# Sliding-window attention and a ReGLU layer: the planner replaced by a written-out sequence, and the second layer of tile 1 by seven block products

## The chip, the core and the metric

The kernel runs on one core of one Trainium2 chip. The metric is the device time of one execution in microseconds (us), of which several runs are taken. A profile of one execution stands beside it: its span runs from the first to the last instruction on the core, and its own time is a little longer than that span. The engines are PE (TensorE, with its weight loads listed apart as PEld), DVE (VectorE), ACT (ScalarE), POOL (GpSimd) and SP (SyncE, which here only issues transfers).

## The reference

Two steps follow each other, with float32 inputs and output.

```python
# q, k, v: [8, 8, 576, 64] (batch, heads, sequence, head size)
scores = 0.125 * q @ k.T                    # per batch and head
mask   = (rel >= 0) & (rel < 64)            # rel = position of query - position of key
attn   = softmax(where(mask, scores, -1e9)) @ v
x      = attn.transpose(0, 2, 1, 3).reshape(4608, 512)
out    = (relu(x @ w_gate) * (x @ w_val)) @ w_out     # w_gate, w_val [512, 1536], w_out [1536, 512]
```

Each query sees itself and the 63 positions before it. The second step is most of the arithmetic: three matrix products over 4608 tokens.

## The kernel before, in words

**Tiles.** The 4608 tokens are cut into 9 tiles of 512 (t = 0 to 8; `LAST` is 8). A tile holds eight windows of 64 queries, and as a batch has nine windows, tile t takes most of its windows from batch t and the rest from its neighbour. Everything on SBUF is float16, apart from the tiles `pr` (128x512 float32, twelve of them) in which partial results wait. PSUM has eight banks of 128x512 float32: seven form the pool "bank", one the pool "bo".

**Attention of a tile** (`attend_tile`). GpSimd loads k and q (`qk_load`, L386), VectorE turns them (`qk_trans`, L392). `score_run` (L416, L424) makes the scores of eight windows for one half of the heads in four banks; ScalarE takes the exponential (L684) into four of the ten tiles `p`. v is loaded by GpSimd's queue in several transfers (`v_load`, L395) into every second window block, and the blocks between are filled from there: by a copy on an engine for batches 0 and 1 (`v_copy`, L647 to L655), and from batch 2 on by a transfer from SBUF to SBUF that SP issues (`v_move`, L659). `value_block` (L430) multiplies the weights with v; the 32 blocks of a tile go into five banks of 7, 7, 7, 7 and 4 (`value_bank`), 28 or 16 small products each. Column 64 of each block is the sum for the softmax: VectorE takes its reciprocal (L699), multiplies (`norm`, L437) and turns the result into `xs`, x transposed (`turn`, L442).

**First layer.** Tile 0 takes it directly (`direct_halves`, L836, for the start; `direct_block`, L789). Tiles 1 to 8 take it by block products (`fast_hidden`, L924): each operand is a 2x2 of blocks, and seven products P1 to P7 of sums and differences of blocks stand in for eight. The x sums are made per tile (`x_form`, L755, on POOL or in part DVE), the sums of w_gate and w_val once (`w_form`, L873, on POOL or DVE). Products that are used twice are copied out of PSUM by ScalarE (`snap`, L933), added by VectorE (`sum`, L940), passed through relu on ScalarE (L949), multiplied on POOL (`mult`, L958) into `g_sb`.

**Second layer.** `output` (L998) does it directly: for each of four groups of 128 tokens, twelve products of 512 columns, an evacuation by ScalarE (L1009) and a 256 KB store by SP (L1013). `fast_output` (L1037) does it by seven block products of 2 x 6 matmuls of 256 columns (L1088): four sums of g (`g_sum`, L1056, DVE, the last of them also POOL), three copies by ScalarE (L1099), three additions by VectorE (`osum`, L1124), an evacuation (L1127) and stores (L1069). It needs sums of w_out, made once (`w_sums`, `wo_form`, L1032, DVE or POOL). In tile 8 the last block leaves in three pieces: 128 KB, 64 KB and 64 KB (L1111, L1116), the second issued by ScalarE's queue, the other two by SP. Which tiles take which form is set by one number:

```python
TF = int(K["TF"])                          # L1133; 2 before
...
if t < TF:
    output(t, lambda sub, j: ..., range(4))
else:
    fast_output(t, lambda i: ...)
```

**What sets the order.** `first_part` is written out by hand. `second_part` builds some 1640 operations with a name, the engines that may run each (with a duration for each), the operations that it follows and the buffers that it takes and gives back. A planner (`Plan`) then goes through modelled time: whenever an engine is free by its model, `pick` takes the ready operation of the smallest key, `grab` gives it buffers, and `emit` issues its instructions. The keys come from the numbers in `K`, with corrections per tile. The planner has its own model of the transfers (`flow`, `transfer`) and of the fetching of PE's instructions (`fetch`). The instructions of each engine run in the order in which they were emitted; between engines they wait on semaphores. Loads share GpSimd's in-order queue, stores and v moves share SP's.

Of the kernel before, what the change touches and what calls it, by code (L numbers as in the profile page):

```python
# [20 lines left out]
K = {"T1": 49.924, "STEP": 29.94, "wo1": 20.947, "wo2": 27.392, "q0": 0.81, "q1": 2.61, "q10": 3.105, "q11": -1.419, "v": -0.6, "v1": -2.289, "ql": 1.41, "qt": 0.88, "qti": 4.69, "vl": 0.91, "vc": 0.04, "vm": 1.83, "e": 7.62, "gap": 3.77, "gap1": 7.386, "r": -6.21, "tn": 1.66, "xf": 4.78, "wf": -35.503, "wfj": -20.847, "sn": 2.67, "su": -2.15, "re": 17.5, "mu": -6.61, "la": -4.79, "o0": 4.313, "o0j": 21.729, "o0s": -0.33, "oo": 0.007, "os": 0.386, "oj": 4.81, "gs": -1.18, "fo": 0.015, "fi": 0.098, "fs": 4.74, "fu": 0.27, "W0": 119.46, "TF": 2, "rs": 5.846, "rv": 1.504, "rt": 0.895, "wl": -5.903, "wln": 11.853, "l0": -6.097, "l1": 7.146, "lv": -0.183, "lvs": 3.345, "wo0": 16.427, "db": -13.173, "di": -0.612, "dv": 3.665, "slack": 0.5, "d2": 2.074, "bl": 9.0, "lv0": 12.142, "d": {'2:xf': -6.976, '2:gap': 2.801, '2:su': -6.005, '3:r': 8.222, '5:tn': 4.276, '6:fi': -0.099, '7:q0': -4.657, '6:su': 3.912, '6:qti': 7.826, '6:mu': 3.718, '7:e': 6.275, '7:r': 4.193, '1:r': 13.271, '2:vl': 6.019, '3:su': 0.149, '6:gs': -0.12, '6:vm': -0.213, '7:qt': -0.899, '6:re': 13.416, '7:qti': -0.543, '7:su': 1.652, '8:v': -2.013, '8:e': -0.256, '0:r': -1.206, '0:fi': 0.02, '1:os': -0.217, '0:mu': 1.725, '2:q0': 1.741, '2:qt': 1.317, '4:e': -3.039, '3:qt': -1.647, '5:fi': -0.024, '4:tn': -0.784, '6:ql': -0.117, '6:os': -0.156, '5:vl': -3.703, '6:gap': -0.68, '7:gap': -0.33, '7:vl': 1.061, '8:gs': 2.641, '8:mu': -3.707, '0:oj': 0.301, '1:xf': 1.119, '0:la': -0.276, '0:e': 0.153, '0:v': -1.992, '0:ql': 0.562, '0:vc': -0.21, '0:os': 0.264, '0:vm': -3.122, '0:gap': -0.425, '0:su': -2.2, '0:fu': 0.645, '0:qti': 2.927, '0:q0': -0.308, '0:fo': 0.017, '0:q1': 1.371, '0:tn': -0.43, '0:gs': 0.145, '0:oo': -0.005, '0:qt': -0.234, '0:vl': -0.08, '1:gap': 3.317, '0:xf': 0.894, '1:su': 0.479, '0:re': 3.598, '1:qt': 0.476, '1:oj': 1.108, '1:qti': -0.592, '1:re': -4.458, '2:v': -0.349, '2:fs': -4.83, '1:sn': -1.051, '1:fs': 0.31, '2:vm': -1.579, '1:fi': -0.01, '1:fo': -0.048, '2:fu': -2.569, '1:v': 0.852, '1:oo': -0.029, '1:q0': 0.371, '2:fo': -0.012, '1:tn': 0.283, '1:mu': 0.421, '2:os': 0.099, '1:e': 1.753, '1:q1': 0.357, '1:ql': 0.301, '2:vc': 0.095, '3:fi': -0.026, '2:ql': -0.412, '3:fo': -0.13, '2:tn': -1.562, '3:tn': 1.005, '2:la': -0.315, '2:mu': -1.84, '3:qti': -1.366, '3:e': 3.975, '3:fs': -0.171, '2:re': 1.299, '2:fi': 0.003, '3:gs': 2.169, '3:sn': -1.944, '2:gs': -0.762, '2:oo': 0.02, '3:q0': 0.206, '2:sn': -0.542, '2:e': 1.079, '3:q1': -0.835, '3:vc': 0.13, '2:q1': 0.676, '3:xf': -0.808, '4:qti': 1.269, '4:v': -0.286, '4:q0': -1.124, '4:la': 0.685, '3:ql': -0.066, '3:vl': -0.069, '3:la': 0.114, '3:mu': -0.69, '3:fu': -0.034, '4:fi': -0.002, '4:fo': -0.035, '4:os': 0.034, '3:re': -1.107, '3:v': -0.668, '3:os': 0.038, '4:q1': -0.644, '4:re': 10.33, '4:fs': 0.147, '4:sn': -0.236, '4:r': -0.56, '5:e': -4.75, '4:mu': -1.436, '5:sn': -0.929, '5:fo': 0.022, '4:fu': 1.111, '5:oj': -0.83, '4:xf': -0.115, '5:v': -3.283, '5:re': 1.853, '5:gs': 1.765, '5:la': 2.425, '5:oo': -0.102, '5:os': 0.039, '4:oj': 0.107, '5:fs': -0.393, '4:oo': 0.002, '5:xf': 0.475, '5:gap': 0.037, '4:gap': 0.009, '4:vm': -0.251, '4:vl': -0.186, '5:vc': -1.079, '5:su': -1.334, '6:xf': -3.246, '6:fo': 0.058, '6:e': 3.933, '5:q1': 0.282, '5:vm': 0.736, '5:fu': 0.612, '6:tn': -0.333, '6:oo': -0.064, '6:q1': 0.038, '6:vc': -0.831, '5:qt': -0.35, '6:fs': -1.242, '5:ql': 0.14, '5:q0': -0.526, '6:vl': -0.535, '6:fu': -0.538, '5:mu': -0.49, '5:r': -0.711, '7:gs': -1.426, '6:v': -0.377, '7:tn': -0.762, '7:oo': 0.079, '7:vm': 0.69, '7:fs': 0.778, '7:fi': 0.0, '6:r': 0.133, '7:v': -1.49, '6:qt': -0.711, '6:q0': -0.395, '7:ql': 0.339, '6:sn': 0.042, '8:su': -1.663, '8:os': 0.104, '8:tn': 1.195, '8:q1': 1.664, '7:fu': -0.818, '7:os': -0.003, '8:fu': -0.594, '7:q1': 0.55, '8:fo': 0.075, '7:mu': -0.507, '7:xf': 0.075, '8:gap': -0.962, '7:vc': 0.072, '8:vm': -0.773, '8:vc': -1.223, '7:sn': 0.05, '8:vl': -0.544, '8:xf': -0.329, '8:oj': -0.046, '7:fo': 0.002, '7:oj': 0.682, '8:qti': -0.921, '8:fs': -1.361, '8:re': -0.296, '8:oo': 0.012, '8:la': 0.307, '7:re': -1.461, '8:fi': 0.008, '8:qt': -0.143, '8:q0': 0.588}, "pads": 78, "cap": 4.8}  # L21


PLANS = []


class Op:


    def __init__(self, name, key, engines, fn, after, take, give, dma):  # L30
        self.small = 0
        self.count = 0
        self.opens, self.closes = None, False
        self.name = name
        self.key, self.engines, self.fn = key, engines, fn
        self.take, self.give, self.dma = take, give, dma
        self.left = len(after)
        self.feeds = []
        self.ready = dict.fromkeys(engines, 0.0)
        self.end = None  # L40
        self.on = None


class Plan:


    LAG = {"PE": 0.055, "ACT": 0.035, "DVE": 0.035, "POOL": 0.075, "SP": 0.06}
    DRAIN = 0.2
    AHEAD = 20.0
    TURN = 0.093  # L50
    LIMIT = 1e9
    FLIGHT = 8
    STAY = 4.0
    ASK = 165
    NEED = 445

    def __init__(self, free, queue, pools):
        self.free = dict(free)
        self.queue = queue
        self.pools = {name: [(t, n, item) for n, (t, item) in enumerate(items)] for name, items in pools.items()}  # L60
        self.home = {id(x[2]): name for name, items in self.pools.items() for x in items}
        self.open = []
        self.known = {e: [] for e in free}
        self.waiting = {e: [] for e in free}
        self.times = []
        self.port = {"DVE": 0.0, "POOL": 0.0}
        self.small = False
        self.at = 0
        self.asked = self.got = 0
        self.come = []  # L70
        self.flight = [None] * self.FLIGHT
        self.moved = 10.0
        self.jobs = {"q": [[10.0, queue["q"] - 10.0, "q", None]], "sp": []}
        self.n = 0
        self.all = []
        self.log = []

    def op(self, name, key, engines, fn, after=(), take=(), give=(), dma=None):
        after = [a for a in dict.fromkeys(after) if a is not None]
        o = Op(name, key, engines, fn, after, take, give, dma)  # L80
        self.n += 1
        o.n = self.n
        self.all.append(o)
        for a in after:
            a.feeds.append(o)
        return o

    def know(self, o):
        for e in o.engines:
            self.known[e].append(o)  # L90
            heapq.heappush(self.times, o.ready[e])

    def fetch(self, n, t, dur, keep):
        at, asked, got, come = self.at, self.asked, self.got, list(self.come)
        end = at + n
        while True:
            ask, need = 256 * asked + self.ASK, 256 * got + self.NEED
            nxt = min(ask, need, end)
            t += (nxt - at) * dur / n
            at = nxt  # L100
            if at == end:
                break
            if ask <= need:
                begin = max([t] + come[-1:])
                begin += max(0.4, min(K["cap"], self.queue["q"] - begin), min(2.0, self.queue["sp"] - begin))
                come.append(begin + 2.4 + K["slack"])
                asked += 1
            else:
                t = max(t, come[got])
                got += 1  # L110
        if keep:
            self.at, self.asked, self.got, self.come = at, asked, got, come
        return t
# [6 lines left out]
    def flow(self, jobs, now, until):  # L120
        done = []
        while now < until and any(jobs.values()):
            act = {w: j[0] for w, j in jobs.items() if j and j[0][0] <= now + 1e-9}
            after = min([until] + [j[0][0] for j in jobs.values() if j and j[0][0] > now + 1e-9])
            if not act:
                now = after
                continue
# [1077 lines left out]
```

## Time and profile before

| | before |
|---|---|
| median of 3 runs | 306.01 us (305.54 to 306.56) |
| the profiled execution: its time | 305.09 us |
| its span | 303.1 us |
| mean granted TensorE clock | 0.997 |
| POOL busy | 231.5 us (76%), 233 instructions |
| HBM read, written | 37.75 MB, 9.44 MB |
| DMA on the whole | 32.87 MB, mean 108 GB/s |

The busy lines and the stages that the prediction rests on are shown there. How to read them: a row of busy times gives what an engine was working on, not whether the end waited for it; the chain of waits, followed back from the last instruction, says that. An engine that is busy 97% of the span can lose time only in the places where its rows have gaps, and most of the gaps of this profile lie ahead of 66 us. Line numbers in the rows are those of the kernel before.

### The profile page before, as it was taken

How to read it: one execution, taken by the hardware profiler on the slowest of the kernel's cores; microseconds unless marked ns; L12 is line 12 of the kernel's file. 1: busy time of each engine (PE TensorE's matmuls, PEld its weight loads, DVE VectorE, ACT ScalarE, POOL GpSimd, SP SyncE). 2: the span in 40 equal slices, each digit the busy share in tenths (PEclk: the TensorE clock that was granted, in tenths of full speed). 3: DMA queues.
4: the chain of work that ended last, by engine and by line, in shares of the span. 5: the costliest groups of instructions: out<-in, count | busy, mean ns of one | idle time of the engine just before them, and what ended most of it. 6: DMA issues, size and time to landing. Idle time of an engine off the chain costs nothing.

```text
span 303.1 us, 11292 instructions
## 1 busy us (share of the span) xinstructions
PE 294.5 (97%) x4793; PEld 242.5 (80%) x4793; DVE 252.6 (83%) x428; ACT 213.1 (70%) x415; POOL 231.5 (76%) x233
## 2 busy tenths in 40 slices
PE   7799999999999999999999999999999999999994
PEld 5576655778767888888888888888888888888884
DVE  5879999999967988998869998889978688776962
ACT  4464426898588788785866987977588858887731
POOL 8698757999997999799558976699559567948630
PEclk9999999999999999999999999999999999999998
DMA  7999999992599916933979835343931112001024
GB/s 216 186 190 205 196 193 218 182 200 44 37 151 155 165 45 83 145 41 53 207 167 114 116 54 98 76 86 36 118 92 38 40 37 69 2 0 37 19 75 151
DMA packets 59586, 32.87 MB, mean 108 GB/s; under 512 B 39440, under 2 KB 54416, under 8 KB 59536
## 3 DMA queue, kind: packets, MB, share of 16 engines
q0 software_dynamic: 46672, 18.29, 51.6%
q1 hardware_dynamic: 12720, 13.80, 14.5%
q8 instruction: 37, 0.61, 0.9%
q14 instruction: 13, 0.11, 0.1%
q10 hardware_dynamic: 144, 0.07, 0.1%
HBM read 37.75 MB, written 9.44 MB: 156 GB/s over the span
## 4 chain that ended last, share of the span: by engine, by line
PE 89%; DMA 7%; DVE 1%; issue 1%; POOL 1%; ACT 0%; SPq 0%; ACTq 0%; DVEq 0%; POOLq 0%
PE bank L924 46%; PE bank L1088 21%; PE bank L998 6%; PE bank L789 5%; PE bank L430 4%; DMA q<-in_q_dram 3%; PE bank L424 2%; DMA v<-in_v_dram 2%; PE bank L836 2%; DMA v<-v 2%; PE bank L416 2%; DVE qT L392 0%; DVE v L512 0%; POOL k L386 0%; POOL v L395 0%
## 5 line engine op out<-in xcount | busy, mean ns | idle before, releaser
L958 POOL TENSOR_TENSOR g_sb<-pr,pr 128x512 f16<-128x512 f32 x96 | 121.1, 1277 | 37.8 <-ACT pr L949 9.1
L940 DVE TENSOR_TENSOR pr<-bank,pr 128x512 f32<-128x512 f32 x144 | 92.4, 680 | 20.2 <-PE bank L924 15.1
L933 ACT COPY pr<-bank 128x512 f32<-128x512 f32 x144 | 80.8, 590 | 23.1 <-PE bank L924 20.6
L924 PE MATMUL bank<-xt,us 128*128 128x256 f16 x384 | 56.1, 273 | 0.1
L924 PE MATMUL bank<-xt,vs 128*128 128x256 f16 x384 | 55.7, 273 | 0.0
L949 ACT ACTIVATE pr<-pr 128x512 f32<-128x512 f32 x72 | 44.9, 638 | 4.7 <-DVE pr L940 4.5
L684 ACT ACTIVATE p<-bank 128x512 f16<-128x512 f32 (+1 forms) x68 | 36.4, 591 | 10.0 <-PE bank L424 9.9
L924 PE MATMUL bank<-xt,wg 128*128 128x256 f16 x288 | 42.8, 273 | 0.1
L924 PE MATMUL bank<-xt,wv 128*128 128x256 f16 x288 | 42.8, 273 | 0.0
L924 PEld LDWEIGHTS <-vs 128*128 128x128 f16 x384 | 37.3, 98 | 5.3
L924 PEld LDWEIGHTS <-us 128*128 128x128 f16 x384 | 36.8, 98 | 5.1 <-issue 0.3
L395 POOL DMA_DIRECT2D v<-in_v_dram x40 | 35.1, 881 | 1.5 <-DMA wo<-in_moe_w_out_dram 1.1
L1088 PEld LDWEIGHTS <-g_sb 128*128 128x128 f16 x336 | 32.5, 98 | 3.9
L1088 PE MATMUL bank<-wo,g_sb 128*128 128x256 f16 x252 | 32.6, 273 | 0.0
L971 ACT ACTIVATE pr<-bank 128x512 f32<-128x512 f32 x48 | 27.5, 602 | 6.1 <-PE bank L924 4.8
L924 PEld LDWEIGHTS <-wv 128*128 128x128 f16 x288 | 27.7, 98 | 4.5
L924 PEld LDWEIGHTS <-wg 128*128 128x128 f16 x288 | 27.7, 98 | 4.1 <-DVE xt L442 0.4
L437 DVE TENSOR_TENSOR xw<-bank,r 128x448 f16<-128x448 f32 (+2 forms) x45 | 25.8, 574 | 1.6
L1088 PEld LDWEIGHTS <-ss 128*128 128x128 f16 x252 | 24.5, 98 | 3.0
L442 DVE STREAM_TRANSPOSE xt<-xw 128x512 f16<-128x512 f16 (+2 forms) x38 | 24.9, 669 | 0.4
L998 PE MATMUL bank<-wo,g_sb 128*128 128x512 f16 x96 | 23.9, 380 | 0.0
L1088 PE MATMUL bank<-ts,ss 128*128 128x256 f16 x168 | 21.8, 273 | 0.0
(103 smaller groups left out, 388.3 us busy)
## 6 DMA issues: line engine op xcount, KB each, us to landing
out_dram<-pr SPq DMA_DIRECT2D x35, 256.0 KB, 2.8
k<-in_k_dram POOLq DMA_DIRECT2D x15, 288.0 KB, 6.5
q<-in_q_dram POOLq DMA_DIRECT2D x15, 288.0 KB, 6.9
v<-in_v_dram POOLq DMA_DIRECT2D x32, 128.0 KB, 5.3
v<-v SPq DMA_DIRECT2D x12, 132.0 KB, 2.7
v<-v SPq DMA_DIRECT2D x24, 66.0 KB, 3.4
wg<-in_moe_w_gate_dram POOLq DMA_DIRECT2D x6, 256.0 KB, 6.6
wv<-in_moe_w_val_dram POOLq DMA_DIRECT2D x6, 256.0 KB, 8.7
```

Of the source, the lines that this page charges most:

```text
L395: nc.gpsimd.dma_start(v16s[b % 2][lo:hi, g, :, 0:64], v[b, :, 64 * g - 64 + lo:64 * g - 64 + hi].rearrange("h p d -> p h d"))
L437: nc.vector.tensor_tensor(x, blocks_of(to, n)[:, :, 0:D].rearrange("p s (c e) -> p s e c", e=2), r[:, :, :, None].to_broadcast([128, n, 2, ...
L442: nc.vector.transpose(xt[:, 2 * hh:2 * hh + 2, c0:c0 + n].rearrange("p e (s c) -> p s e c", c=32), x)
L684: nc.scalar.activation(pp[g][:, 0:n].rearrange("p n c -> p (n c)"), st[g][:, 0:64 * n], ACT.Exp, scale=scale)
L924: nc.tensor.matmul(slot[to][:, HT * m:HT * m + HT], w[:, kk, 128 * m:128 * m + 128], x[:, kk], start=(first and m == 0 and kk == 0), stop= ...
L933: lambda e, hold=hold, slot=slot: nc.scalar.copy(hold["x"], slot["A"]),
L940: nc.vector.tensor_tensor(hold["x"], slot[to], hold["x"], ADD)
L949: lambda e: nc.scalar.activation(hold["x"], hold["x"], ACT.Relu), after=[o])
L958: lambda e: VEC[e].tensor_tensor(gh[:, fs:fs + 2, h], pair(a["x"]), pair(b["x"]), MUL),
L971: lambda e, hold=hold, slot=slot, i=i: nc.scalar.activation(hold["x"], slot["A"], ACT.Copy if i else ACT.Relu),
L998: nc.tensor.matmul(bank["b"][:, 0:c1 - c0], gs[t % 2][:, f, 128 * sub:128 * sub + 128], wo[:, f, c0:c1], start=(j == 0 and i == 0), stop=( ...
L1088: nc.tensor.matmul(bank[to][:, HD * m:HD * m + HD], a[:, f, 128 * m:128 * m + 128], b[:, f], start=(first and m == 0 and f == 0), stop=(f ...
```

## The change

The planner is gone. In its place stands a string `ORDER` of 1641 steps. A step is the number of an operation (in the order in which the code creates them), a letter for the engine that runs it (P, A, D, G for POOL, S for SP), and a digit for each buffer that it takes. `Plan.run` walks through the string, asserts that everything that an operation follows has been issued and that its buffers are free, and issues it. So the order on every engine, the engine of each operation that may run on several, and the buffers are all written out.

`TF` goes from 2 to 1: tile 1 takes its second layer by seven block products too, so that `output` is left for tile 0 alone and the sums of w_out are needed one tile earlier. The other numbers in `K` change as well; under the written order they only feed keys that nothing reads. `value_bank` can put two banks in one operation, which the number `pair` = 0 leaves off, and the number of tiles `p` is now read from `K` (ten, as before). `first_part` and the bodies of all operations are as they were.

The written order differs from the planner's on every engine. Counted in operations: the five value banks of each tile and the two of tile 0 stand in 18 separate stretches on PE where there were 29; of the 24 sums of w_gate and w_val, 15 run on DVE and 9 on POOL (18 and 6 before), of the 12 sums of w_out 7 and 5 (4 and 8), of the 32 x sums 6 and 26 (8 and 24), and of the copies of v, ScalarE makes 6 (3) and DVE 2 (5). On PE the second operation after the hand-written part is now the second half of a contraction of tile 0 whose first half stands ahead of it. On SP the last steps are the 64 KB piece (step 1640), two 256 KB stores (1628, 1618) and the 128 KB first piece (1636); the planner had the 64 KB piece last.

```diff
-    LAG = {"PE": 0.055, "ACT": 0.035, "DVE": 0.035, "POOL": 0.075, "SP": 0.06}
...
-    def fetch(self, n, t, dur, keep):
...
-    def transfer(self, o, t):
...
-    def pick(self, e, t):
...
-    def run(self, emit):
-        self.todo = sorted((o for o in self.all if "PE" in o.engines), key=lambda o: (-o.key, -o.n))
...
-                for e in ("PE", "ACT", "DVE", "POOL", "SP"):
...
-                    o = self.pick(e, t)
...
-                    self.finish(o, e, begin, dur)
...
+ORDER = """
+29S 2G 30S 3G 36P0 31S 11G 32S 12G 33S 38P 42P4 0G 16P5612 34S 49P3 35S 1G 20Ag 18Ah 48P2 7G 40Ai 43P6 6G 45P 54P7 4G
...
+1601D 1458P 1604D 1609D 1616P 1605D 1459P 1607D 1606D 1619P 1603D 1460Am 1456D 1620P 1461S 1453S 1622P5 1610D 1621Ao
+1457S 1602D 1275S 1623P 1611D 1443S 1625P 1624As 1626P 1629P 1627D 1630P 1617D 1633P 1631D 1634P 1635Ai 1632S 1637A
+1639D 1638A 1640S 1628S 1618S 1636S
+"""
...
     def run(self, emit):
+        at = {id(x): n for n, x in enumerate(self.items)}
+        steps = ORDER.split()
+        assert len(steps) == len(self.all)
+        for step in steps:
+            n = 0
+            while step[n].isdigit():
+                n += 1
+            o, e, items = self.all[int(step[:n])], self.LETTERS[step[n]], [self.DIGITS.index(x) for x in step[n + 1:]]
+            assert not o.done and all(a.done for a in o.after) and e in o.engines
+            for pool, holder, names in o.take:
+                for name in names:
+                    x = items.pop(0)
+                    assert self.home[x] in pool.split("+")
+                    self.spare.remove(x)
+                    holder[name] = self.items[x]
+            emit(o, e)
+            o.done = True
+            self.spare.update(at[id(holder[name])] for _, holder, name in o.give)
...
-        plan = Plan({"PE": 14.4, "ACT": 16.65, "DVE": 17.5, "POOL": 13.7, "SP": 3.0},
-                    {"q": 17.0, "sp": 3.0},
...
+        plan = Plan({"bank": banks[:7], "bo": banks[7:], "p": ps, "pr": prs})
...
-        SIZES = (7, 7, 7, 7, 4)
+        SIZES = ((7, 7), (7, 7), (4,)) if K["pair"] else ((7,), (7,), (7,), (7,), (4,))
...
-        end = plan.run(emit)
-        return plan
+        plan.run(emit)
```

More of the change, by code (lines that the diff above doesn't have):

```diff
@@ L27, with __init__ @@
+1639D 1638A 1640S 1628S 1618S 1636S
+"""
 class Op:
[L30 removed]
+    def __init__(self, name, engines, fn, after, take, give):
         self.small = 0
@@ new lines, in __init__ @@
+        self.engines, self.fn, self.after = engines, fn, after
+        self.take, self.give = take, give
+        self.done = False
+class Plan:
+    LETTERS = {"P": "PE", "A": "ACT", "D": "DVE", "G": "POOL", "S": "SP"}
+    DIGITS = "0123456789abcdefghijklmnopqrstuvwxyz"
+    def __init__(self, pools):
+        self.items = [x for items in pools.values() for x in items]
+        self.home = [name for name, items in pools.items() for _ in items]
+        self.spare = set(range(len(self.items)))
@@ L686, in attend, with value_bank @@
             return pp, exps
-        def value_bank(t, key, parts, before, gives, last):
+        def value_bank(t, key, groups, before, gives, last):
             to = {}
-            m = len(parts)
-            s0 = parts[0][0]
+            every = [part for parts in groups for part in parts]
             def run(e):
-                for i, (_, pp, win, hh, at, s) in enumerate(parts):
-                    value_block(to["b"], VW * i, pp, win, hh, at, s)
-            def recip(e):
-                nc.vector.reciprocal(rw[t % 2][:, s0:s0 + m], blocks_of(to["b"], m)[:, :, D:D + 1])
-            def normed(e):
-                norm(to["b"], m, xw[:, s0:s0 + m], rw[t % 2][:, s0:s0 + m])
-            after = [o for part in parts for o in windows_v(part[2])] + before
-            a = op("values", key, pe(0.031 * m), run, after=after, take=[("bank", to, ("b",))], give=gives)
-            a.small = a.count = 4 * m
-            for b in {part[2] // NG for part in parts}:
-                value_ops[b].append(a)
-            r = op("recip", key + kt("r"), {"DVE": (0.17, False)}, recip, after=[a])
-            return a, op("norm", key + kt("r") + 0.3, dve(64 * m), normed, after=[r] + last, give=[("bank", to, "b")])
@@ new lines, in run @@
+                for n, parts in enumerate(groups):
+                    for i, (_, pp, win, hh, at, s) in enumerate(parts):
+                        value_block(to[n], VW * i, pp, win, hh, at, s)
+            after = [o for part in every for o in windows_v(part[2])] + before
+            a = op("values", key, pe(0.031 * len(every)), run, after=after, take=[("bank", to, range(len(groups)))], give=gives)
+            a.small = a.count = 4 * len(every)
+            for b in {part[2] // NG for part in every}:
+                value_ops[b].append(a)
```

348 lines of the change are left out of this document (103 added, 245 removed).

## The prediction

> **What bounds the kernel now.** I read the page's busy line and chain first, then a table by stage, then the chain in order of time and the timelines of TensorE and of SyncE's queue.
>
> ```profile
> PE 294.5 (97%) x4793; PEld 242.5 (80%) x4793; DVE 252.6 (83%) x428; ACT 213.1 (70%) x415; POOL 231.5 (76%) x233
> PE 89%; DMA 7%; DVE 1%; issue 1%; POOL 1%; ACT 0%; SPq 0%; ACTq 0%; DVEq 0%; POOLq 0%
> ```
>
> ```profile
> 40.00:50.00 10.00, 9.31 (x176) 5.22 (x175) 9.73 (x18) 3.66 (x8) 4.70 (x7) 1.00 1.42 198
> 50.00:60.00 10.00, 9.83 (x208) 7.41 (x207) 9.78 (x17) 8.29 (x16) 9.81 (x12) 1.00 1.37 196
> 60.00:66.00 6.00, 5.91 (x166) 4.71 (x165) 5.97 (x10) 5.45 (x11) 5.55 (x7) 1.00 1.02 186
> 260.00:290.00 30.00, 30.00 (x277) 26.87 (x276) 22.35 (x36) 23.31 (x44) 21.78 (x18) 1.00 0.06 19
> ```
>
> The columns are stage, length, then busy time of PE, weight loads, DVE, ACT, POOL. PE works without a break from 66 to 299 us. Between 40 and 66 it waits a little (0.95 us idle, more inside rows), DVE is full (25.5 of 26 us), and the DMA queues carry nearly 200 GB/s. So three things can move the end: PE's own work, the stretch up to 66 us, and what follows PE's last product (299.3 to 303.1).
>
> ```profile
> 53.31 5.99 DMA v<-in_v_dram
> 59.99 5.50 DMA v<-v
> 75.50 0.86 PE bank L998 x4
> 126.26 1.31 PE bank L1088 x12
> 287.49 11.80 PE bank L1088 x108
> ```
>
> In the chain: four 512-wide products take 0.86 us (216 ns each), twelve 256-wide ones 1.31 (109 each). The two DMA rows are the wait for tile 2's v: the load lands at 59.3, the move of its rows at 65.5, and only then does the second value bank of tile 2 run.
>
> ```profile
> 114.84 0.82 PE L1088 MATMUL bank<-wo,g_sb 128*128 128x256 f16 x6
> 115.59 0.40 PE L430 MATMUL bank<-v,p 128*32 128x65 f16 x28
> 115.91 0.61 PE L924 MATMUL bank<-xt,wv 128*128 128x256 f16 x4
> 121.56 0.82 PE L1088 MATMUL bank<-ts,ss 128*128 128x256 f16 x6
> 122.31 0.67 PE L430 MATMUL bank<-v,p 128*32 128x65 f16 x56
> 122.91 0.61 PE L924 MATMUL bank<-xt,us 128*128 128x256 f16 x4
> ```
>
> A stretch of value products costs the time to the next big row, less the six products before it (6 x 0.109 = 0.65): 28 products 115.91 - 114.84 - 0.65 = 0.42 us, 56 together 122.91 - 121.56 - 0.65 = 0.70. Two apart cost 0.84, so each separate start costs 0.14.
>
> ```profile
> 14.47 0.82 PE L836 MATMUL bank<-xt,wg 128*128 128x192 f16 x8
> 15.12 0.82 PE L836 MATMUL bank<-xt,wv 128*128 128x192 f16 x8
> 15.98 1.66 PE L836 MATMUL bank<-xt,wg 128*128 128x192 f16 x16
> ```
>
> ```profile
> 293.38 5.72 SPq L1069 DMA_DIRECT2D out_dram<-pr  x5
> 299.76 0.84 SPq L1116 DMA_DIRECT2D out_dram<-pr  x2
> out_dram<-pr SPq DMA_DIRECT2D x5, 256.0 KB, 2.2
> out_dram<-pr SPq DMA_DIRECT2D x1, 64.0 KB, 1.7
> ```
>
> The first fence is PE's start on tile 0, used below. The second is the end: five 256 KB stores leave SP between 293.4 and 299.1, two small pieces end its queue at 300.6, and the last lands at 300.25 + 1.7 = 302.0, 1.1 before the span's end.
>
> **The change part by part.** (1) *Tile 1's second layer as block products.* Removed: 48 products of 512 columns, 48 x 0.216 = 10.37 us of PE, and 4 evacuations (ACT). Added: 84 of 256, 84 x 0.109 = 9.16; four sums of g (DVE, L1056, 0.78 to 0.89 each), three snapshots and an evacuation (ACT, 0.59), three additions (DVE, 0.685). PE: -1.2 us. The 5.4 us of DVE lie beside PE between 66 and 110, where DVE has slack: 80 to 110 had 24.9 of 30 busy. If that cover went, each DVE microsecond too many would stop PE for as long.
>
> A rule speaks against this part. The Trainium skill ("TensorE: Matmul & The Clock Gate", section "Back-to-back issue gap") says that real streams run at about 131 ns a product at 512 columns and 81 at 128. My estimate from that page for 256 is 98, so the change would cost 84 x 98 - 48 x 131 = +1.9 us. The rows with 216 and 109 contradict it.
>
> (2) *Fewer small stretches.* In the written order the 42 value groups stand in 18 stretches, not 29, and PE turns to small products 34 times, not 37. Some of the eleven joins only put values next to scores or split such a pair, worth less than 0.14. Adding up PE's small stretches by the rows' prices (scores 0.93, 28 values 0.42, 56 0.70, 72 0.85) gives 28.0 us against 29.2 before without its stalls: -1.2 us; bounds -0.8 and -1.5 (11 x 0.14).
>
> (3) *PE's start.* The second instruction group is now the second half of tile 0's contraction, which ran at 15.98 in before; four 192-wide products end at 14.8. PE stands 1.2 us with everything queued behind (scores included), and a little later it waits for gate weights whose load stands as early in POOL's queue as before and landed at 20.4 there. By then I count 1.85 us of stall, against 0.5 to 0.7 before (rows at 15.98 to 20.8). After that the loads, in their new queue order and at before's 1.26 us for each 256 KB, land before PE asks.
>
> (4) *40 to 66 us.* Before lost about 1.8 us here: 0.9 at 43 to 44, where PE's values waited for a copy of v, 0.6 at 53 to 55 and 0.3 at 65. In the new order tile 1's v loads are issued earlier and the first of these goes. But tile 1's direct products, which filled gaps from 65 on, are gone, and the chain is kept: first-tile values, v loads, moves by SP, second value bank of tile 2. It begins at about 50.5, as before (1.85 us of early stall stand for 1.7). POOL now does an x sum (1.16 us) ahead of the third v load; against this only one k/q load is issued beside the moves, not three (59.28 to 60.97 in before). A move took 5.5 us beside those. I take the value bank at 64.5; the ends are 63.3 (no wait at all) and 65.9 (moves as slow as before). DVE agrees: its queue up to the sum that PE needs 3.0 us of its own work after that bank is 2.4 us shorter (three weight sums, three v copies, a k turn and an x turn fewer, three output-weight sums more). DVE is full here, so that sum ends at 69.3 - 2.4 = 66.9 at best, which puts the bank at 63.9. Stall here 1.2 us, ends 0 and 2.6.
>
> (5) *Later.* Loads, sums and products of the eight tiles are reordered. Before has no PE wait here; three v moves now stand 0.5 to 1.5 us nearer to their use (tiles 3, 5, 6), behind stores in SP's queue. I take 0.4 us, ends 0 and 1.0.
>
> (6) *The end.* SP's queue now closes differently: after the last 64 KB piece, which must wait for the last evacuation, it still issues two 256 KB stores and the 128 KB first piece, whose data are ready up to 1.9 us earlier. Before issued those ahead. SP issues such stores 0.46 to 0.5 apart, so they leave at 300.65, 301.1 and 301.6 on before's clock; neighbours at such distances landed up to 2.7 us after issue. The last lands at 303.6 to 303.9 instead of 302.0: +1.7 us, nothing hides it; ends 1.3 (128 KB alone, 1.8 to land) and 2.2.
>
> **Sum.** PE's work -1.2 - 1.2 = -2.4; stalls 1.85 + 1.2 + 0.4 = 3.45 against 2.35 before: +1.1; end +1.7. Together +0.4 us. The profiled execution took 305.09 (span 303.1 and 2.0 around it), which becomes 305.5; it stands 0.92 below the median of 306.01, so I forecast **306.4**.
>
> **The rivals.** *A, forecast, 0.40*: gain on PE and loss at both ends cancel. A time within 0.3% (0.92 us, what a measurement of this kernel can tell from no change) is counted as the same.
>
> *B, slower, 0.31*: the stretch from 50 to 70 us is bound by DMA and DVE, not by PE, so shorter PE work there buys nothing. It decides once the second value bank of tile 2 starts after 65.5, as in before: stall 2.4 instead of 1.2, and with 0.6 more in (5) the time is 306.4 + 1.8 = **308.2**. For it: DVE 5.97 of 6 us and the two DMA rows. Against it: the shorter DVE queue and fewer k/q loads.
>
> *C, faster, 0.27*: the moves run free (2.1 to 2.4 us each, as those at 82 to 85 do) and the bank starts when PE gets there: -1.2, (5) costs nothing: -0.4, the closing stores 1.5 instead of 1.7: 306.4 - 1.8 = **304.6**. Against it: SP now issues a move that waits for the third load ahead of one that could go.
>
> *D, 0.02*: the seven products save no PE time; then 306.4 + 1.2 = **307.6**. The 109 ns row speaks against it. This is the case of the Trainium skill's rule above; its figures would give 306.4 + 1.2 + 1.9 = 309.5 as an estimate.
>
> **Range.** With every term at its good end: work -1.2 - 1.5, stalls 1.85 - 2.35 = -0.5, end +1.3, together -1.9, so 304.1. With every term at its bad end: work -1.2 - 0.8, stalls 5.45 - 2.35 = +3.1, end +2.2, together +3.3, so 309.3. From C to B, with 0.3 on either side for the terms that each leaves at its middle, **304.3 to 308.5** leaves out no more than 2 in 10. Faster 0.27 (C), same 0.40 (A), slower 0.33 (B and D).
>
> **What would show it.** (1) 672 products of the seven-product kind where there were 588, and 48 of 512 columns where there were 96. (2) Rows of 56 and 72 value products at every tile. (3) A gap of PE of over 1 us at 14.8. (4) Tile 2's second value bank at 64.5 instead of 65.5. (5) PE busy 30 of 30 us in every window after 70. (6) Three stores on SP behind the last 64 KB piece, and 5.5 us instead of 3.8 from PE's last product to the span's end. I am wrong if PE waits after 70 us, if the early stretch hands on more than 1.2 us of gain, or if the closing stores cost under 1.3 us.

## The result, and the profile after

The changed kernel takes 309.32 us (median of 4 runs, 308.45 to 310.13), the kernel before 305.77 beside it: a ratio of 1.0116, with an interval of 1.0073 to 1.0158. It is 3.5 us slower. The forecast of 306.4 and its range up to 308.5 were both too low. The profiled execution took 309.82 us, with a span of 307.6, 4.5 more than that of before.

The busy line and the chain by engine, from the page of the changed kernel:

```profile
PE 294.2 (96%) x4829; PEld 246.5 (80%) x4829; DVE 248.2 (81%) x430; ACT 213.2 (69%) x418; POOL 234.1 (76%) x235
PE 88%; POOL 4%; DMA 4%; DVE 1%; issue 1%; ACT 0%; SPq 0%; DVEq 0%; ACTq 0%; POOLq 0%
```

PE is busy as long as before, but in a longer span. The table by stage (columns as in the prediction: PE, weight loads, DVE, ACT, POOL; then PE's granted clock, the mean DMA share and GB/s) says where the rest is:

```profile
40.00:50.00 10.00, 9.91 (x179) 5.42 (x178) 8.03 (x17) 5.95 (x9) 7.12 (x9) 1.00 1.34 203
50.00:60.00 10.00, 9.71 (x208) 7.11 (x206) 9.67 (x18) 8.41 (x18) 9.14 (x10) 1.00 1.23 194
60.00:66.00 6.00, 4.13 (x124) 3.30 (x123) 4.05 (x8) 3.73 (x8) 3.90 (x5) 1.00 0.94 142
66.00:80.00 14.00, 13.23 (x221) 11.06 (x208) 11.05 (x23) 9.98 (x19) 11.32 (x10) 0.88 0.18 35
260.00:290.00 30.00, 30.00 (x277) 26.89 (x275) 19.80 (x29) 22.91 (x44) 23.88 (x20) 1.00 0.03 10
```

Between 40 and 50 it goes better than before (9.91 against 9.31). Between 60 and 66 PE loses 1.9 us, DVE, full in before, idles for a third of the time, and ACT and POOL are not full either (3.73 and 3.90 of 6 us): this points to a late transfer. From 66 to 80 the granted clock is 0.88; before, that stage was full and at full clock:

```profile
66.00:80.00 14.00, 14.00 (x180) 11.04 (x179) 13.32 (x25) 10.85 (x21) 13.47 (x13) 1.00 0.48 71
```

From 80 to 290 PE works without a break, as forecast.

PE's timeline around tile 2's value products (L296):

```profile
62.38 0.30 PE L296 MATMUL bank<-v,p 128*32 128x65 f16 x16
64.56 0.28 PE L296 MATMUL bank<-v,p 128*32 128x65 f16 x12 [1.87 <-DMA v<-v]
...
66.14 0.21 PE L296 MATMUL bank<-v,p 128*32 128x65 f16 x4
67.12 0.52 PE L296 MATMUL bank<-v,p 128*32 128x65 f16 x24 [0.77 <-DMA v<-v]
67.58 1.04 PE L791 MATMUL bank<-xt,us 128*128 128x256 f16 x4
68.41 1.06 PE L791 MATMUL bank<-xt,wv 128*128 128x256 f16 x4
69.26 1.06 PE L791 MATMUL bank<-xt,us 128*128 128x256 f16 x4
70.11 0.64 PE L791 MATMUL bank<-xt,vs 128*128 128x256 f16 x4
```

Both value banks wait for the moves of v rows, to 64.56 and to 67.12. Before, the first did not wait, and the second had only a short wait inside its row:

```profile
62.53 0.40 PE L430 MATMUL bank<-v,p 128*32 128x65 f16 x28
65.11 0.68 PE L430 MATMUL bank<-v,p 128*32 128x65 f16 x28
```

From the first value products of a bank to the next big row it is now 2.38 us (62.38 to 64.76) and 1.44 us (66.14 to 67.58), where 28 products took 0.33 in before (62.53 to 62.86): this costs 3.2 us. Then three rows of four products follow each other at 0.84 us instead of 0.44. PE's granted clock is 0.50 from 66.8 to 70.1. The three rows cost another 1.2 us; with the value products ahead of them, which ran at half clock too, the clock costs about 1.4.

The chain of waits of the changed kernel leads to that place:

```profile
56.54 1.15 POOL xt L622
57.70 1.14 POOL ts L899
58.90 1.16 POOL ts L899
60.06 0.88 POOL v L261
60.93 0.56 POOL q L252
61.50 1.20 POOL wo L899
62.71 0.49 SPq L519
63.30 3.78 DMA v<-v
```

It reads as if the last v load of tile 2 (L261) came too late, behind an x sum and two sums of w_out on GpSimd's queue, with a move behind it. That was my first theory, and it fell.

PE's start and SyncE's end, from the timelines:

```profile
14.51 0.49 PE L703 MATMUL bank<-xt,wg 128*128 128x192 f16 x4 [0.24 <-DVE xt L308]
16.02 0.83 PE L703 MATMUL bank<-xt,wg 128*128 128x192 f16 x8 [1.02 <-DMA wg<-in_moe_w_gate_dram]
```

```profile
295.84 5.72 SPq L936 DMA_DIRECT2D out_dram<-pr  x6
302.71 0.34 SPq L983 DMA_DIRECT2D out_dram<-pr  x1
303.11 0.96 SPq L936 DMA_DIRECT2D out_dram<-pr  x2
304.16 0.43 SPq L983 DMA_DIRECT2D out_dram<-pr  x1
```

PE stands 1.2 us at 14.8, and SyncE issues three stores behind the last 64 KB piece, the last at 304.16. PE's last product ends at 301.7, so 5.9 us follow it (3.8 before).

### The profile page after: what moved, and what is told of

It reads as the page before. It is cut to its first block, busy times and chain, and to the rows that moved or that the text cites. A ratio compares the mean times of both kernels' runs of the same rounds, so it can differ in the third digit from the quotient of the medians.

```text
span 307.6 us, 11292 instructions
## 1 busy us (share of the span) xinstructions
PE 294.2 (96%) x4829; PEld 246.5 (80%) x4829; DVE 248.2 (81%) x430; ACT 213.2 (69%) x418; POOL 234.1 (76%) x235
## 3 DMA queue, kind: packets, MB, share of 16 engines
q0 software_dynamic: 46672, 18.29, 50.8%
q1 hardware_dynamic: 13232, 13.80, 14.4%
## 4 chain that ended last, share of the span: by engine, by line
PE 88%; POOL 4%; DMA 4%; DVE 1%; issue 1%; ACT 0%; SPq 0%; DVEq 0%; ACTq 0%; POOLq 0%
PE bank L791 46%; PE bank L955 24%; PE bank L656 5%; PE bank L296 3%; PE bank L865 3%; PE bank L290 3%; DMA wg<-in_moe_w_gate_dram 2%; PE bank L703 2%; PE bank L282 2%; DMA v<-v 1%; POOL v L261 1%; POOL ts L899 1%; DVE xw L303 1%; POOL wo L899 0%; POOL xt L622 0%
## 5 line engine op out<-in xcount | busy, mean ns | idle before, releaser
L807 DVE TENSOR_TENSOR pr<-bank,pr 128x512 f32<-128x512 f32 x144 | 94.4, 682 | 24.8 <-PE bank L791 19.1
L791 PE MATMUL bank<-xt,us 128*128 128x256 f16 x384 | 57.1, 276 | 0.1
L544 ACT ACTIVATE p<-bank 128x512 f16<-128x512 f32 (+1 forms) x68 | 36.5, 593 | 16.1 <-PE bank L290 16.1
L955 PEld LDWEIGHTS <-g_sb 128*128 128x128 f16 x384 | 37.3, 98 | 4.4
L955 PE MATMUL bank<-wo,g_sb 128*128 128x256 f16 x288 | 36.7, 273 | 0.0
L261 POOL DMA_DIRECT2D v<-in_v_dram x40 | 35.3, 884 | 1.9 <-DMA wg<-in_moe_w_gate_dram 1.0
L955 PEld LDWEIGHTS <-ss 128*128 128x128 f16 x288 | 27.9, 98 | 3.3
L955 PE MATMUL bank<-ts,ss 128*128 128x256 f16 x192 | 24.9, 273 | 0.0
L258 DVE STREAM_TRANSPOSE qT<-q 128x576 f32<-128x576 f32 x16 | 19.9, 1245 | 0.9 <-DMA q<-in_q_dram 0.8
```

Source lines behind the costliest of these rows:

```text
L258: nc.vector.transpose(dst.rearrange("p (i j) -> p j i", i=32), src)
L261: nc.gpsimd.dma_start(v16s[b % 2][lo:hi, g, :, 0:64], v[b, :, 64 * g - 64 + lo:64 * g - 64 + hi].rearrange("h p d -> p h d"))
L544: nc.scalar.activation(pp[g][:, 0:n].rearrange("p n c -> p (n c)"), st[g][:, 0:64 * n], ACT.Exp, scale=scale)
L791: nc.tensor.matmul(slot[to][:, HT * m:HT * m + HT], w[:, kk, 128 * m:128 * m + 128], x[:, kk], start=(first and m == 0 and kk == 0), stop= ...
L807: nc.vector.tensor_tensor(hold["x"], slot[to], hold["x"], ADD)
L955: nc.tensor.matmul(bank[to][:, HD * m:HD * m + HD], a[:, f, 128 * m:128 * m + 128], b[:, f], start=(first and m == 0 and f == 0), stop=(f ...
```

## The experiments

Each edit is made in the written sequence of the changed kernel unless said otherwise; the diffs show the steps of the engine concerned. Ratios are to the kernel before, timed beside each run (e_tail, e_sp, e_pool and e_vchain beside 305.87 us; e_late, e_early, e_after and p_tf1 beside 305.37; e_lt, e_lts and p_afterK beside 305.50; e_kq beside 305.31). Runs that were timed beside different medians are best compared by their ratios.

### The closing stores (e_tail)

```diff
 SyncE:
-1632S 1640S 1628S 1618S 1636S
+1628S 1618S 1632S 1636S 1640S
```

> The changed kernel, with only the last steps of SyncE's queue in another order: the two 256 KB stores and the 128 KB piece leave as soon as their data are there, and the last 64 KB piece closes the queue, as before the change. Theory (the closing order costs 1.3 to 2.2 us, step 6 of the prediction): the last piece leaves at about 302.7 as now, lands at 304.3, the span ends 3.8 us behind TensorE's last product and not 5.9, and the time is 309.3 - 1.9 = 307.4. Rival (the 0.9 MB of closing stores are bound by their transfer, in whatever order): the last landing stays near 306.5, and the time at 309.3.

Measured: 307.22 us, ratio 1.0049 (1.0006 to 1.0093), against 1.0116. SyncE's queue at the end of this kernel:

```profile
293.90 5.72 SPq L936 DMA_DIRECT2D out_dram<-pr  x8
300.29 0.84 SPq L983 DMA_DIRECT2D out_dram<-pr  x2
```

The two small pieces close the queue again; from PE's last product to the end it is 4.0 us, where it was 5.9. The eight runs lie between 305.52 and 309.07, so that the size rests on these two traces, and on e_lt and e_late below, which differ in the closing stores alone and are 1.9 us apart. Step 6 was right: the closing order costs about 2 us.

### One swap on SyncE, one on GpSimd, and both (e_sp, e_pool, e_vchain)

```diff
 SyncE, v moves of tile 2 (e_sp, e_vchain):
-356S 359S 357S 360S 364S
+356S 357S 359S 360S 364S
 GpSimd (e_pool, e_vchain): the last v load (361) and tile 3's first k load (532) change places
-354G 355G 196G 358G 362G 532G 199G 314G 316G 361G 534G 307G 209G
+354G 355G 196G 358G 362G 361G 199G 314G 316G 532G 534G 307G 209G
```

> The changed kernel, with one swap on SyncE's queue: the v move that waits only for the first two loads of tile 2 now leaves ahead of the one that waits for the third load. Theory 1 (order on the in-order queues: the last loads of v are issued too late on GpSimd's queue, so the swap alone frees little): the swapped move leaves at about 58 instead of 63.3, but the next value products still wait for the move of the third load's rows, to about 66.9: 309.3 - 0.2 = 309.1 (308.6 to 309.3). Theory 1b (the head of SyncE's queue is the whole of it): the second wait of PE (0.95 us at 66.1 to 67.1) and the slow clock behind it go, -2.3: 307.0. Theory 2 (rival B of the prediction: 50 to 70 us is bound by DMA and VectorE): 309.3, no change.

> The changed kernel, with one swap on GpSimd's queue: the last v load of tile 2 (issued at 60.0, behind a k load, an x sum and two sums of w_out) changes places with the k load of tile 3 (issued at 55.6). Same work, same bytes, VectorE untouched. Theory 1 (the order on GpSimd's queue makes tile 2's v late): the load leaves at 55.6, the loads have landed by 61.5, the moves by 64, PE's waits of 1.95 and 0.95 us between 62 and 67 shrink to 0.3 or less, and the stretch of half clock behind them (1.4 us lost) goes: 309.3 - 3.9 = 305.4 (304.8 to 306.5). Theory 2 (rival B: the stretch is bound by DMA and VectorE): the same bytes land no sooner, bank at about 67 as now: 309.3 (308.8 to 309.8).

> The changed kernel with both swaps, that on GpSimd's queue and that on SyncE's. Theory 1: the ready move leaves at 57.5 to 58 as well, no wait of PE over 0.1 us is left between 60 and 70 and the granted clock there is 1.00: 309.3 - 4.1 = 305.2 (304.6 to 306.2). Theory 2 (bound by DMA and VectorE): 309.3. If this equals the run with the swap on GpSimd's queue alone, the head of SyncE's queue costs nothing once the loads are early.

Measured: e_sp 307.67, ratio 1.0072 (1.0038 to 1.0105), between the two forms of theory 1; e_pool 312.17, ratio 1.0216 (1.0169 to 1.0264); e_vchain 309.81, ratio 1.0139 (1.0081 to 1.0197). In its trace the swapped move of e_sp left at 60.05, but it landed at 66.84, no sooner than in the changed kernel (66.88). That execution ran about 1 us later by then (its first v load of tile 2 left at 51.8 instead of 50.8), so the trace alone does not show what the swap gained. Bringing the last v load forward by 4 us made the kernel slower, with the swap on SyncE (e_vchain against e_sp) as without it (e_pool against the changed kernel). These two results refute theory 1, which the chain had suggested, and theory 2 as well: the bytes were the same, yet the time moved. Some of e_pool's time is clock: its trace has half clock from 15.9 to 19.3, far ahead of the edit, and from 67.1 to 73.9. The DMA view of e_vchain, for the issues between 60.8 and 62.4 (number, size, median time to landing), shows what changed:

```profile
q<-in_q_dram POOLq DMA_DIRECT2D x1, 288.0 KB, 5.5
v<-v SPq DMA_DIRECT2D x2, 66.0 KB, 5.3
```

All five v loads had landed by 62.0, but a k and a q load now ran beside the moves, which took 5.3 us for 66 KB; PE waited 1.97 us for them. In e_pool the moves beside these loads took up to 6.2 us. This gave theory 3.

### The k and q loads behind the moves (e_late, e_kq)

```diff
 GpSimd:
-362G 532G 199G 314G 316G 361G 534G 307G 209G
+362G 361G 199G 314G 316G 307G 209G 532G 534G      e_late (with the swap on SyncE)
+362G 199G 314G 316G 361G 307G 209G 532G 534G      e_kq (nothing else)
```

> The changed kernel with the ready v move first on SyncE's queue, the last v load of tile 2 early on GpSimd's (as in the run with both swaps), and now the k load and the q load of tile 3 behind all of them, at about 64 to 66 instead of 60.6 and 61.1. Theory 3 (the moves of v rows are slow because k or q loads run beside them: 4.9 to 6.2 us with a k load beside, 2.3 to 3.5 without): the moves that leave at 61 to 62.5 take 2.3 to 3 us and land by 65, PE's waits for v between 62 and 68 are under 0.5 us together, and the time is 309.3 - 4.0 = 305.3 (304.5 to 306.5). Theory 2 (the v loads and moves are bound by their own packets, whatever lies beside them): moves still land at 66.5 to 68, PE waits 2 us and the time is 308.5 to 310.

> The changed kernel with one edit: the k load and the q load of tile 3 go behind the next product of g on GpSimd's queue, from 55.6 and 61 to about 63 to 64. The last v load of tile 2 stays behind the two sums of w_out, the ready v move stays behind the waiting one on SyncE's queue, the closing stores stay as changed. Theory 3 in its strong form (the k and q loads beside the v loads and moves are the whole of the loss at 62 to 70): 309.3 to 310.3 falls to 306 (305.3 to 306.8), as with all three edits (305.85). Theory 3 in its weak form (the head of SyncE's queue and the place of the last v load cost as well, once the k and q loads are gone): 307.3 (306.8 to 308.3). Theory 1 alone (only the order of the v loads and moves counts): 309 to 310.

Measured: e_late 305.85, ratio 1.0023 (1.0002 to 1.0044); e_kq 306.69, ratio 1.0042 (1.0023 to 1.0060). Both lie where theory 3 put them, e_kq with its strong form. e_late differs from e_vchain in the place of the k and q loads alone, 3 us later: 4.0 us faster by the medians, 3.5 by the ratios. The same DMA view of e_late, then the first move of tile 2 (132 KB) in the changed kernel, and the moves of e_kq, the 132 KB one being that same first move:

```profile
v<-v SPq DMA_DIRECT2D x3, 66.0 KB, 2.0
```

```profile
v<-v SPq DMA_DIRECT2D x1, 132.0 KB, 7.0
```

```profile
v<-v SPq DMA_DIRECT2D x3, 66.0 KB, 3.2
v<-v SPq DMA_DIRECT2D x1, 132.0 KB, 2.5
```

Among tile 2's moves, those that left with neither a k nor a q load ahead of them took 1.9 to 3.6 us (e_late, e_kq), and those with one ahead 3.4 to 7.0 (the changed kernel, e_vchain); two in e_tail took 2.3 and 2.9 even so. The single landings show why the place counts: as a rule, a move that left while loads issued ahead of it were on their way landed just behind them. In e_vchain the k and q loads issued at 60.55 and 61.14 landed at 64.73 and 66.61; the move issued at 61.20 had its first packet at 64.5 and landed at 66.68. In e_late the last load ahead landed at 62.69, and the moves issued at 61.80 and 62.38 landed at 63.73 and 64.38.

PE's waits in e_kq shrink to 0.64 us, and its clock from 66 to 80 is 1.00. So the k and q loads account for about 3.1 us of the loss (309.8, the mean of the two medians of the changed kernel, to 306.69), or 2.8 by the ratios. The swap on SyncE with the earlier load would make some 0.8 more, but the intervals of e_kq and e_late overlap, so this is not shown. The parts do not add up either: e_sp, the swap alone, was some 2 us better than the changed kernel.

### Earlier v loads (e_early)

The five v loads and their moves in the order of e_late, but the loads ahead of two sums of w_out:

```diff
 GpSimd:
-310G 312G 354G 355G 196G 358G 362G 532G 199G 314G 316G 361G 534G 307G 209G
+354G 355G 358G 362G 361G 310G 312G 196G 199G 314G 316G 307G 209G 532G 534G
```

> The changed kernel with all five v loads of tile 2 issued as soon as their buffer is free (about 46 to 50 on GpSimd's queue, 4.7 us sooner, ahead of two sums of w_out instead of behind them), the ready v move first on SyncE's queue and the k and q loads of tile 3 behind. Theory 3 (the loads are bound by their packets, about 2 us for each 128 KB, so that only an earlier start helps, and a free queue for the moves): the loads land at 54 to 60, the moves by 62.5, PE has no wait for v between 60 and 70 and the granted clock there is 1.00: 309.3 - 4.5 = 304.8 (304.0 to 305.8). Theory 2 (VectorE, full in this stretch, bounds it): the loads land sooner, but PE's products of tile 1 or the value banks wait for VectorE instead: 307 to 309.

Measured: 306.81, ratio 1.0040 (1.0005 to 1.0075): no better than e_late, and not the 304.8 of theory 3. The waits for v are gone, but PE stands elsewhere, as its timeline and the DMA view of 51.5 to 54 (first e_early, then the changed kernel; packets, MB, and the time of the packets as a share of 16 engines' time, over 100% where packets overlap) show:

```profile
55.45 0.38 PE L791 MATMUL bank<-xt,wv 128*128 128x256 f16 x2 [0.16 <-ACT p L544]
57.36 0.39 PE L791 MATMUL bank<-xt,wv 128*128 128x256 f16 x2 [1.53 <-issue]
```

```profile
q0 software_dynamic: 2573, 0.38, 214.9%
q1 hardware_dynamic: 19, 0.04, 4.0%
```

```profile
q1 hardware_dynamic: 243, 0.46, 53.5%
q0 software_dynamic: 443, 0.07, 37.8%
q8 instruction: 1, 0.02, 4.7%
```

The wait of 1.53 us has "issue" as its cause: no semaphore. In the changed kernel a transfer of instructions (q8, 16 KB) starts at 51.6; in e_early GpSimd's queue (q0) is full of v packets then, and the transfer starts at 55.0 and ends at 56.0, 1.4 us before PE goes on at 57.36. I read this as PE waiting for its own program behind the v loads. Other traces agree: their "issue" gaps of 0.3 us and more, e_late 0.89 at 70.81, e_after 0.37 at 18.37, e_lts 0.94 at 18.38 and p_tf1 1.00 at 125.63, all end 1.3 to 1.5 us after such a transfer has ended. Neither theory had it; it was not tried apart.

The moves of e_early correct theory 3 in one point. The first four had only v loads ahead, the last of which landed at 61.23; they took 4.1 to 6.3 us and landed at 61.41 to 61.94. In p_afterK, below, the first four moves took 3.2 to 4.7 us behind v loads. So v loads hold up a move as k and q loads do; in the changed kernel it was a k and a q load that stood ahead without need.

### The changed kernel again, and the block products under the planner (e_after, p_tf1, p_afterK)

p_tf1 is the kernel before with `TF` = 1, p_afterK the kernel before with all of the changed kernel's numbers `K`; both keep the planner.

```diff
-K = {"T1": 49.924, ..., "W0": 119.46, "TF": 2, ...}
+K = {"T1": 49.924, ..., "W0": 119.46, "TF": 1, ...}      p_tf1
+K = {"T1": 48.443, ..., "W0": 64.57, "TF": 1, ...}       p_afterK
```

> The changed kernel once more, unedited, beside the others: 309.3 by its first runs (308.4 to 310.1). If it comes out at 307.7 or less here, the swap on SyncE's queue alone has bought nothing.

> The kernel before with its planner, and TF = 1 instead of 2 as the only edit: tile 1's second layer by block products, in an order that the planner finds with the numbers of before. If the block products save what the prediction says (1.2 us of PE, with VectorE's 5.4 us covered): 306.0 - 1.2 = 304.8, 304 to 306.5 with what the planner shifts. If the block products themselves are what made the changed kernel slower (VectorE's sums, or sums of w_out that come too late or crowd out the v loads): 307 or more.

> The planner of the kernel before with the numbers of the changed kernel (TF = 1 and all tuned keys with it): tile 1's second layer by block products, without the written order. If the written order is what lost (its queues on GpSimd and SyncE, its closing stores): the planner's plan has stores closing as before and k and q loads spaced by its model of the queue, so 304 to 306.5. If the block products in tile 1 lose by themselves (VectorE or the w_out sums get in the way): 308 or more.

Measured: e_after 310.30, ratio 1.0149 (1.0112 to 1.0186), against which the swap on SyncE alone (e_sp, 1.0072) is a gain, though its interval overlaps that of the changed kernel's first runs (1.0116); p_tf1 321.07, ratio 1.0492 (1.0455 to 1.0530); p_afterK 305.35, ratio 0.9989 (0.9961 to 1.0016). p_tf1 missed its aim. Its longest wait of PE is

```profile
PE bank L1088 <- DVE ss L1056: 3.0, 1, 3.0
```

that is, for a sum of g, in the last tile (at 307.7). In all PE idles 10.4 us behind 14.4 us, where it idled 1.0 in before. I take it that the due times in `K`, made for direct products in tile 1, do not fit; this was not tried apart. With numbers made for it, the planner does the block products in the time of before. So the block products did not make the changed kernel slow; the written order did. But they bought nothing visible under that planner either (-0.1%, where 1.2 us of PE would be 0.4%, the very edge of the interval). The traces show where it went: from the first direct product at 14.5 us to the last product, PE's time without its idle gaps fell from 283.8 to 282.7 us, and its idle gaps grew from 1.0 to 1.7.

### Both repairs, and PE's start (e_lt, e_lts)

e_lt is e_late with the closing stores of e_tail. e_lts also has another start:

```diff
 PE:
-36P0 38P 42P4 16P5612 49P3 48P2 43P6 45P 54P7 44P 56P 51P 84P0 55P7 57P 37P4 39P 76P0 88P1 21P5 24P6 50P 68P1 80P7
+36P0 42P4 43P6 38P 44P 16P5312 54P7 48P2 49P3 45P 56P 50P 51P 55P7 57P 37P4 39P 84P0 76P0 88P1 21P5 24P6 80P7 68P1
```

> The changed kernel with the k and q loads of tile 3 behind tile 2's v moves (as in the run at 305.85) and the closing stores in the order of their data (as in the run at 307.22). Theory (the two losses are separate and add up): the first was worth 3.5 to 4.5 us, the second 2.05, so 305.85 - 2.05 = 303.8 (303.0 to 304.5), below the kernel before (305.4 to 306.0) by 0.5% to 0.7%. Rival (the stores of the end are held up by something else once PE ends sooner): 305 to 306.

> The same, and PE's start in an order that has more to do at 14.8: three first halves of tile 0's contraction, then the second halves and the scores, all halves ahead of the next weights' blocks. Theory (step 3 of the prediction: 1.2 us of PE's stall at 14.8 can be had back, less 0.6 that goes to the second gate block, which lands at 24.5 whatever PE does): 303.8 - 0.6 = 303.2. Rival (loads of weights set the pace up to 25 us, so a denser start only waits later): 303.8, no change.

Measured: e_lt 303.96, ratio 0.9948 (0.9920 to 0.9977), faster than both kernels and close to the 303.8 expected; the two losses are separate and add up. Its busy line and two of its stages:

```profile
PE 291.9 (97%) x4829; PEld 245.8 (81%) x4829; DVE 248.4 (82%) x430; ACT 213.1 (71%) x418; POOL 233.8 (77%) x235
```

```profile
60.00:66.00 6.00, 6.00 (x170) 4.98 (x168) 5.75 (x12) 5.53 (x12) 4.79 (x6) 1.00 0.63 113
66.00:80.00 14.00, 14.00 (x194) 12.27 (x192) 13.28 (x24) 11.53 (x23) 13.93 (x13) 1.00 0.28 49
```

PE has no gap from 60 to 80, and its busy time is 2.6 us less than before. Of this 0.4 lies in the first 14 us, which are as they were; from 14.5 us to the last product and without idle gaps PE takes 281.5 us, where it took 283.8 before. The 2.3 between them are close to the 2.4 that steps 1 and 2 forecast. e_lts took 304.85, ratio 0.9968 (0.9938 to 0.9997), and not the 303.2 expected; it lies nearer to its rival (303.8). The gap at 14.8 became smaller, but two others came, as PE's timeline shows:

```profile
18.38 0.20 PE L290 MATMUL bank<-qT,kT 32*128 32x64 f16 x2 [0.94 <-issue]
...
23.83 1.46 PE L656 MATMUL bank<-xt,wg 128*128 128x384 f16 x8 [0.58 <-ACT pr L666]
```

The first is again an "issue" gap, the second a wait for a bank that an activation had not yet left. I read PE's gap at 14.8 as time in which such waits had been hidden; this was not tried apart.

## Why the prediction was wrong

| step | forecast, us | in the profiled execution |
|---|---|---|
| (1) block products, PE | -1.2 | -1.2: 672 products instead of 588, 48 of 512 columns instead of 96 |
| (2) fewer small stretches | -1.2 | about -1.1: with (1), PE's time from 14.5 us on, without idle gaps and half clock, is 281.5 us, 283.8 before |
| (3) stall to 24 us | 1.85 | 1.5 |
| (4) stall 40 to 66 us | 1.2 | 0.3 + 0.8 + 3.2, and 1.4 of half clock: 5.7 |
| (5) later stalls | 0.4 | 0 |
| stalls of before | -2.35 | -2.35 |
| (6) the end | +1.7 | +2.05 |
| sum | +0.4 | +4.5 by the span (307.6 against 303.1); the rows give 4.6 |

The parts of step 4 are read from starts of rows and overlap by about 0.1 us. Five of the six steps came within 0.4 us. **Step 4 failed**, at "I take the value bank at 64.5; the ends are 63.3 (no wait at all) and 65.9 (moves as slow as before)". The first value bank waited to 64.56 and the second ran at 67.12, outside these ends. Three things were wrong in it.

First, I counted the k and q loads beside the moves ("against this only one k/q load is issued beside the moves, not three") as if fewer were better, and took before's 5.5 us as the worst that a move could take, though two later moves of before took 6.2 and 7.5. There were two, not one: the k load issued at 55.6 landed only at 64.06, and the q load was issued at 60.9. The first move left at 57.5, behind that k load, landed at 64.51 and so took 7.0 us. What counts is which loads are queued when the move is issued: e_vchain and e_late carry the same loads, and 3 us in the place of two of them are worth 3.5 to 4.0 us.

Second, "DVE agrees" was no support. I bounded the bank by DVE's queue, but DVE idled for 1.95 of 6 us there. A shorter queue on an engine says nothing about a transfer that it waits for.

Third, no case had a price for the clock. The wait was taken to cost its own length; here 1.4 us came on top, though not in every execution. It was lost in rows without a gap (67.6 to 70.1), although the reading given ahead of the prediction says that so busy an engine can lose time only where its rows have gaps. In the four runs the mean clock was 0.991, 0.997, 0.996 and 0.992, and the two low ones are the two longest times (309.82 and 310.13 against 308.45 and 308.82). That agrees, but does not show it for the runs without a profile, as the mean also falls when the clock halves at the end: in the profile of e_after, with waits of 0.75 and 1.17 us in this place, the clock stayed at 1.00 here and the mean was 0.994.

Of the rivals, B named the place and the row (the moves of v) and the side, but priced it at 308.2, because its bank was at 65.5 as in before. Its reason, that DMA and DVE bound the stretch, is only half right: the v moves were bound by the loads that had been issued ahead of them, and changing places freed 3.5 to 4 us without a byte less. D is refuted: the products cost 109 ns, and under the planner (p_afterK) nothing was lost. C's condition, moves of 2.1 to 2.4 us, is nearly what e_late brought about for the last three moves (1.9 to 2.5). Two numbers of the prediction lie at the measured 309.32 by chance: the sum with every term at its bad end (309.3), because only step 4 failed and went far beyond its bad end, and the 309.5 given with D, though the products took 109 ns, as the forecast had it.

## What to carry to other kernels

Before costing a reordered queue, write down for each transfer on the critical chain which loads have been issued ahead of it and have not landed: a 66 KB move took 2.0 us with hardly any left ahead (e_late) and 5.3 behind a k and a q load (e_vchain), so a load that nobody needs yet belongs behind the moves that PE is about to wait for. The chain of waits names an order of events, not a cause: bringing forward the v load that stood in the chain made the kernel slower (312.17), while holding back a k load that did not stand there, and the q load behind the v load, made it faster (306.69). And a store that is ready belongs ahead of one that still waits: three stores behind a waiting one at the end of an in-order queue cost 2 us that nothing hides.

## What the runs showed of the hardware

- SBUF-to-SBUF moves of v rows (66 or 132 KB, on SyncE's queue) took 1.9 to 2.5 us when the loads issued ahead of them on GpSimd's queue had landed or landed within 1 us (e_late, e_lt). Otherwise most landed just behind those loads: after 3.4 to 7.0 us behind k or q loads (the changed kernel) and after 4.1 to 6.3 behind v loads alone (e_early). The Trainium skill ("DMA: Bandwidth & Descriptors", section "Queues, rings and completion order") says that each DMA engine takes turns between the queues that have work, packet by packet. This case's trace agrees only in part: in e_vchain packets of the q load and of the moves run side by side from 64.5 to 66.0, but the move issued at 61.20 had no packet before 64.5, while packets of the k load, issued at 60.55, ran from 61.8 on. Why it had none is open.
- Waits of 1.87 and 0.77 us within 5 us were followed by half clock (four products in 0.84 us instead of 0.44), granted from 66.8 to 70.1; with 0.64 us of waits (e_kq) the clock in that stage was 1.00. The length of a wait alone does not decide it: in e_pool a wait of 1.04 us that ended at 16.1 went with half clock from 15.9 to 19.3, while at the same place the changed kernel, e_vchain, e_late, e_kq, e_early and e_lt kept full clock with waits of 1.02 to 1.20 us. The Trainium skill ("TensorE: Matmul & The Clock Gate", section "HAM oscillation — how this bites in real kernels") gives as its rule no idle gap over about 3.4 us; here the longest wait was 1.87 us, and the clock fell all the same. The halving itself agrees with the page.
- PE stood 1.53 us (e_early) and 0.94 us (e_lts) without any semaphore. In e_early a 16 KB transfer of instructions started 3.4 us later than in the changed kernel (55.0 against 51.6). These gaps, and three more in e_late, e_after and p_tf1, ended 1.3 to 1.5 us after such a transfer had ended. It reads as PE being stopped by its own program; no run tried this apart.
